# A delta-rule attention with two FFNs on one core: two weights' norms as traces on TensorE, keys and key grams in another form, small products kept together, and a new issue order

## The chip, the cores and the metric

One core of one Trainium2 chip runs the kernel. The metric is device time in microseconds (us), from runs on the chip; the profile is one execution recorded by the hardware profiler. Its engines are called PE (matrix products; PEld is its weight load), DVE (vector operations), ACT (scalar activations), POOL and SP (which issues the DMAs).

## The reference

A delta-rule attention with B = 4, H = 8, S = 768, D = 48 gives x; two FFN layers with 384 → 2048 → 384 follow. Cut to what is computed:

```python
k_n = k / (np.linalg.norm(k, axis=-1, keepdims=True) + 1e-06)
state = np.zeros((B, H, D, D))
for t in range(S):
    y[:, :, t] = einsum('bhd,bhde->bhe', q[:, :, t], state)
    v_old = einsum('bhde,bhd->bhe', state, k_n[:, :, t])
    state += beta[:, :, t, None, None] * einsum('bhd,bhe->bhde', k_n[:, :, t], v[:, :, t] - v_old)
x = y.transpose(0, 2, 1, 3).reshape(B * S, H * D)      # 3072 x 384
h = x @ w_in;  x = np.maximum(0.01 * h, h) @ w_out     # first FFN
h = x @ w2_in; x = (h - np.tanh(h)) @ w2_out           # second FFN
```

## The kernel before

**Work and tiles.** The sequence is cut into 12 chunks `n` of 64 steps; two chunks make a pair `u`. A chunk's attention works on 32 (batch, head) matrices at once: the keys are normalized and transposed (`keys`, `t_batch`: `kf`, `kt`), their gram gives `gd` and `AT` (`g_batch`), 32x32 triangular blocks are inverted on DVE (`inverses`: one stream transpose, then 30 steps of two operations on `xi` and `gd`, then two transposes into `XW`), two rounds of 32x32 products put the corners in (`merges`: products `gd,AT`, `XW,AT`, then `XW,PM`, `PM,gd`), and `queries`, `products`, `states` and `outputs` make the chunk's x. These products are small: 48 or 64 rows by 48 or 64 columns, several of them beside each other in the array, 32 products to a batch. An f32 product goes to PE as two pieces.

**The FFNs.** Each chunk gives 256 tokens. `to_xa` scales them by a power of two from their sum of squares (a norm product `ab,ones` on PE adds over the partitions), splits them into f16 hi and lo, and transposes both. `h_part` makes `ps_h` with three f16 products (hi·hi, hi·lo, lo·hi) per block, ACT and DVE make the activation's halves `g`, `o_part` adds into `ps_o`. `to_xb` does for the second layer what `to_xa` does for the first. The order of layers is 0 and 0 of a pair of chunks, then 1 and 1.

**The weights.** Four weights (0 to 3) are loaded as 64-bit words, unpacked on DVE (`w_f32`, tiles `wi` and `wo`: a shift and two operations of 128x768 for two column blocks), squared with a running sum on ACT (`square_sum` into `wacc`), and, once all 16 blocks are there, scaled by a power of two, `sw` (`pow2_scale`), and split into hi (ACT, then a DMA) and lo (DVE, `wo<-wo,sw,sx`). For weight 0, PE makes the lo half from a scaled unit matrix (`unit_s`) and ACT copies it back. `weight` already has a branch for weights in `TRACE`, which is empty here: it takes the upper 16 bits of the f32 words as bf16,

```python
top = o.bitcast(BF16).rearrange("p (b n w) -> p b n w", n=128, w=2)[:, :, :, 1]
for b in range(w * KT):
    mm(ps, top[:, b], top[:, b], traced == 0, traced == NF * KT - 1)
...
tt(diag, ps, ident, ALU.mult)
dve("tensor_reduce", out=acc[:, 0:1], in_=diag, axis=AX.X, op=ALU.add)
```

so that the diagonal of 48 accumulated 128x128 products holds the sums of squares.

**What sets the order.** All operations are first put into a graph (`put`, `matmul`). `schedule` is a list scheduler: it goes through a model of the engines with costs per instruction, and gives each engine its whole order. Priorities come from the longest tail of work behind an operation plus an offset per stage, the table `BIAS` (some 270 numbers, `("weight", 0, 3)` for a quarter of weight 0's split, and so on). Tiles come from rings of buffers (`sx`, six rooms; `ps_a`, four small PSUM banks; `ps_h` and `ps_o`, two each), and the scheduler lets a tile in when a room is free. On the chip each engine works through its list in order and waits on semaphores. The constants `K_DMA` (chunks whose keys are transposed by DMA), `M8` (pairs whose merges use eight instead of four tiles of the array) and others switch parts on for some chunks.

Of the kernel before, what the change touches and what calls it, by code (L numbers as in the profile page):

```python
# [30 lines left out]
def layers(n):  # L31
# [12 lines left out]
TRACE = ()  # L44
K_SUM = ()
GQ = range(12)
FLIP = range(2, 12)
K_DMA = range(2, 12)
# [19 lines left out]
    ('dma', 'o_part1', 8): -53.43, ('dma', 'o_part1', 9): -2.8, ('dma', 'products', 1): -76.55,  # L68
    ('dma', 'products', 10): -3.83, ('dma', 'products', 2): 25.34, ('dma', 'products', 3): -131.98,
    ('dma', 'products', 4): -6.69, ('dma', 'products', 5): -26.09, ('dma', 'products', 6): 19.17,  # L70
    ('dma', 'products', 7): 77.49, ('dma', 'products', 8): 212.34, ('dma', 'products', 9): 68.97,
    ('dma', 'queries', 0): -146.73, ('dma', 'queries', 1): 17.69, ('dma', 'queries', 10): -116.19,
    ('dma', 'queries', 11): 10.95, ('dma', 'queries', 2): -28.97, ('dma', 'queries', 3): -147.71,
    ('dma', 'queries', 4): -53.56, ('dma', 'queries', 5): 11.09, ('dma', 'queries', 6): -62.06,
    ('dma', 'queries', 7): 5.92, ('dma', 'queries', 8): -44.59, ('dma', 'queries', 9): 63.43,
    ('dma', 'to_xa', 1, 1): -72.81, ('dma', 'to_xa', 10, 1): -8.26, ('dma', 'to_xa', 11, 1): 154.84,
    ('dma', 'to_xa', 2, 1): 2.93, ('dma', 'to_xa', 3, 1): 5.4, ('dma', 'to_xa', 4, 1): 32.04,
    ('dma', 'to_xa', 5, 1): 3.58, ('dma', 'to_xa', 6, 1): 16.44, ('dma', 'to_xa', 7, 1): -144.99,
    ('dma', 'to_xa', 8, 1): -22.03, ('dma', 'to_xa', 9, 1): 22.28, ('dma', 'to_xb', 0, 1): -131.12,
    ('dma', 'to_xb', 1, 1): -169.83, ('dma', 'to_xb', 10, 1): -107.58, ('dma', 'to_xb', 11, 1): 50.71,  # L80
    ('dma', 'to_xb', 2, 1): -7.15, ('dma', 'to_xb', 3, 1): -6.01, ('dma', 'to_xb', 4, 1): -20.2,
    ('dma', 'to_xb', 5, 1): 65.65, ('dma', 'to_xb', 6, 1): -16.83, ('dma', 'to_xb', 7, 1): -97.29,
    ('dma', 'to_xb', 8, 1): 34.46, ('dma', 'to_xb', 9, 1): -4.63, ('dma', 'v', 0): -65.53,
    ('dma', 'weight', 0, 0): -46.39, ('dma', 'weight', 0, 1): -40.51, ('dma', 'weight', 0, 2): -23.2,
    ('dma', 'weight', 0, 3): 21.56, ('dma', 'weight', 0, 4): 56.7, ('dma', 'weight', 0, 5): -5.62,
    ('dma', 'weight', 1, 0): -159.92, ('dma', 'weight', 1, 1): -183.08, ('dma', 'weight', 1, 2): -28.75,
    ('dma', 'weight', 1, 3): -35.61, ('dma', 'weight', 1, 4): -172.45, ('dma', 'weight', 1, 5): -164.56,
    ('dma', 'weight', 2, 0): -32.76, ('dma', 'weight', 2, 1): -6.37, ('dma', 'weight', 2, 2): 4.29,
    ('dma', 'weight', 2, 3): -15.49, ('dma', 'weight', 2, 4): -23.36, ('dma', 'weight', 2, 5): -0.69,
    ('dma', 'weight', 3, 0): 5.74, ('dma', 'weight', 3, 1): -258.17, ('dma', 'weight', 3, 2): -95.47,  # L90
    ('dma', 'weight', 3, 3): -26.22, ('dma', 'weight', 3, 4): 24.43, ('dma', 'weight', 3, 5): -55.49,
# [524 lines left out]
def kernel(  # L616
# [473 lines left out]
    def inv_eng(u):  # L1090
        return INV
# [420 lines left out]
```

## Time and profile before

| | |
|---|---|
| device time, median of 3 runs | 966.23 us (964.88 to 966.59) |
| profiled execution, its own time | 965.78 us |
| its span in the profile | 963.6 us |
| PE busy, products | 896.5 us (93%), 12756 |
| DVE busy, instructions | 608.6 us (63%), 1332 |
| ACT busy, instructions | 499.5 us (52%), 1187 |
| DMA | 71.30 MB, mean 74 GB/s |

The profiled execution's time is 2.2 us above its span, which begins with the first and ends with the last recorded instruction. Busy time is a sum over the span; products of PE overlap, and their ends are modelled.

### The profile page before, as it was taken

The page shows a single profiled execution, that of the slowest core. Times are in us where ns is not written, and L with a number is a line of the kernel's source. Part 1 is how long each engine was busy: PE and PEld are TensorE (multiplying, and loading weights), DVE is VectorE, ACT ScalarE, POOL GpSimd, SP SyncE. Part 2 cuts the span into 40 slices and gives each one's busy share as a digit, 9 for nine tenths or more (in the row PEclk, how much of TensorE's full clock was granted, in tenths as well). Part 3 has the DMA queues.
Part 4 walks back from the last instruction along what each step waited for, and adds up shares of the span by engine and source line. Part 5 has one row for each costly group of instructions (what it writes and reads, how often), then busy time and mean ns, then how long its engine had stood idle before and what let it go on. Part 6 is the DMA issues. An engine that isn't in the chain of part 4 may idle for free.

```text
span 963.6 us, 29002 instructions
## 1 busy us (share of the span) xinstructions
PE 896.5 (93%) x12756; PEld 677.5 (70%) x12756; DVE 608.6 (63%) x1332; ACT 499.5 (52%) x1187; POOL 4.9 (1%) x22
## 2 busy tenths in 40 slices
PE   2346899999999999999999999999999999999997
PEld 2215777778777777777777777777777768777675
DVE  7999999987984458953253598499322344512342
ACT  7657767666357566346362427544334434524342
POOL 1000000000000000000000000000000000000000
PEclk9586799999999999999999999999999999999999
DMA  9983673325022432121012111212021000300000
GB/s 349 402 235 104 193 181 116 108 67 95 23 74 59 71 90 64 21 56 36 18 41 33 55 41 36 50 31 56 17 56 18 3 19 17 52 1 18 17 18 16
DMA packets 86718, 71.30 MB, mean 74 GB/s; under 512 B 61760, under 2 KB 73024, under 8 KB 86592
## 3 DMA queue, kind: packets, MB, share of 16 engines
q1 hardware_dynamic: 86592, 69.46, 27.1%
q8 instruction: 99, 1.62, 0.7%
q14 instruction: 27, 0.22, 0.1%
HBM read 44.14 MB, written 4.72 MB: 51 GB/s over the span
## 4 chain that ended last, share of the span: by engine, by line
PE 79%; DVE 13%; ACT 4%; issue 2%; DMA 1%; SPq 1%; ACTq 0%; DVEq 0%
PE ps_h L609 36%; PE ps_o L609 35%; PE ps_a L609 8%; DVE xi L612 3%; DVE wo L612 3%; DVE wi L612 3%; DVE gd L612 2%; ACT gd L612 1%; DVE g L612 1%; DMA wo<-in_w_in_dram 1%; ACT sx L612 1%; DVE sx L612 1%; ACT XW L612 1%; ACT jk L612 1%; ACT wo L612 1%
## 5 line engine op out<-in xcount | busy, mean ns | idle before, releaser
L609 PE MATMUL ps_h<-x,wi 128*128 128x256 f16 x3456 | 403.6, 273 | 3.1 <-ACT sx L612 2.6
L609 PE MATMUL ps_o<-wo,g 128*128 128x384 f16 x2304 | 400.9, 326 | 0.2 <-issue 0.2
L609 PEld LDWEIGHTS <-wi 128*128 128x128 f16 x3456 | 334.9, 98 | 57.3 <-issue 4.5
L609 PEld LDWEIGHTS <-g 128*128 128x128 f16 x2304 | 221.9, 98 | 132.9 <-issue 0.5
L612 ACT ACTIVATE g<-sx 128x512 f16<-128x512 f32 x192 | 120.3, 628 | 113.0 <-PE ps_o L609 57.6
L612 DVE TENSOR_TENSOR g<-sx,g 128x512 f16<-128x512 f32 x96 | 66.0, 688 | 112.6 <-ACT g L612 112.0
L612 DVE SCALAR_TENSOR_TENSOR sx<-sx,kap,ps_h 128x512 f32<-128x512 f32 x96 | 71.2, 744 | 66.8 <-ACT sx L612 66.3
L612 ACT ACTIVATE sx<-ps_h 128x512 f32<-128x512 f32 x96 | 56.7, 592 | 91.8 <-PE ps_h L609 63.2
L612 ACT ACTIVATE sx<-ps_h,kap 128x512 f32<-128x512 f32 x96 | 65.1, 681 | 73.7 <-PE ps_h L609 63.4
L612 DVE SCALAR_TENSOR_TENSOR g<-sx,g 128x512 f16<-128x512 f32 x96 | 66.0, 688 | 36.4 <-ACT g L612 36.0
L612 DVE TENSOR_TENSOR gd<-xi 128x30 f32<-128x30 f32 (+9 forms) x180 | 59.2, 329 | 3.5
L612 DVE TENSOR_TENSOR xi<-xi,gd 128x30 f32<-128x30 f32 (+9 forms) x180 | 59.1, 329 | 3.5
L612 ACT ACTIVATE jk<-kf 128x48 bf16<-128x48 f32 x160 | 38.4, 240 | 14.3 <-DMA kf<-in_k_dram 10.7
L612 ACT ACTIVATE sx<-x,sxs 128x768 f16<-128x768 f32 (+1 forms) x26 | 22.7, 881 | 22.1 <-DVE sxs L612 22.1
L612 ACT ACTIVATION_READ_ACCUMULATOR jk<-kf 128x1 f32 x160 | 30.0, 187 | 0.0
L612 DVE SCALAR_TENSOR_TENSOR wi<-wo,wi 128x768 int32<-128x768 int32 x32 | 29.8, 950 | 0.0
L609 PE MATMUL ps_a<-q,kt 48*64 48x64 f32 x768 | 15.1, 229 | 13.8 <-DMA q<-in_q_dram 11.4
L612 DVE SCALAR_TENSOR_TENSOR sx<-x,sxs,sx 128x768 f16<-128x768 f32 (+1 forms) x26 | 24.6, 951 | 4.6 <-ACT sx L612 4.4
L612 ACT ACTIVATE sx<-x 128x768 bf16<-128x768 f32 x24 | 20.2, 840 | 13.7 <-DVE x L612 13.4
L612 ACT ACTIVATE gd<-ps_a 32x256 f32<-32x256 f32 (+1 forms) x72 | 23.9, 373 | 5.2 <-PE ps_a L609 4.6
L609 PEld LDWEIGHTS ps_a<-q,kt 48*64 48x64 f32 x768 | 13.3, 142 | 16.6 <-ACT wo L612 11.5
L612 DVE TENSOR_SCALAR sx<-ps_o,kap 128x384 f32<-128x384 f32 x12 | 7.4, 618 | 27.5 <-PE ps_o L609 25.5
(124 smaller groups left out, 730.2 us busy)
## 6 DMA issues: line engine op xcount, KB each, us to landing
wo<-in_w_in_dram SPq DMA_DIRECT2D x32, 384.0 KB, 7.8
q<-in_q_dram SPq DMA_DIRECT2D x12, 512.0 KB, 4.5
wi<-in_w_out_dram SPq DMA_DIRECT2D x14, 384.0 KB, 7.8
kf<-in_k_dram SPq DMA_DIRECT2D x12, 384.0 KB, 3.4
vf<-in_v_dram SPq DMA_DIRECT2D x12, 384.0 KB, 3.4
out_dram<-sx SPq DMA_DIRECT2D x48, 96.0 KB, 2.2
x<-in_w_out_dram SPq DMA_DIRECT2D x10, 384.0 KB, 4.0
b<-in_beta_dram SPq DMA_DIRECT2D x6, 512.0 KB, 4.7
```

The source lines that it names most:

```text
L609: self.eng["pe"].matmul(out=o.real(), lhsT=lhsT.real(), rhs=rhs.real(), start=start, stop=stop)
L612: getattr(self.eng[n.on], op)(**{k: v.real() if isinstance(v, View) else v for k, v in kw.items()})
```

## The change

Two sets and two ranges are changed, and with them the costs and all offsets; some stages are written anew:

- `TRACE = (0, 1)`: the sums of squares of weights 0 and 1 come from 48 products each on PE, in banks of `ps_h` and `ps_o`, a masked multiplication and a sum on DVE; 16 squares each leave ACT, and one instead of 16 small `wacc,ones` products adds over the partitions.
- `K_DMA` begins at 4: chunks 2 and 3 have their keys transposed by PE products with the unit matrix and PSUM copies, as chunks 0 and 1 did, instead of an f16 split, DMA transposes and an addition.
- `PAIRS`: in chunks 4 to 11 the gram of the keys is three f16 products per tile, of the two halves as the DMA left them, instead of one f32 product. The two f16 tiles live until then.
- `to_xa` takes one scale per half of the tokens, from the partition's own sum, so its norm product over the partitions falls away; `to_xb` multiplies it out, `kappa` has one factor less.
- `schedule`: from some point of the model's time on (`t > 250`), where PE is in the small tiles already and FFN products would come next, a small group that is ready and whose instructions are fetched in time goes first.
- `merges` for pairs 0 and 1 goes half by half.
- Costs `SMALL` get two entries, and every number of `BIAS` is new.

`SPLIT`, `BY_PE` and `K_POOL` are empty, so their branches add nothing; they are left out below.

```diff
-TRACE = ()
+PAIRS = range(4, 12)
+TRACE = (0, 1)
-K_DMA = range(2, 12)
+K_DMA = range(4, 12)
...
-    ('weight', 0, 0): -1.81, ('weight', 0, 1): 28.14, ('weight', 0, 2): 11.71, ('weight', 0, 3): -89.58,
...
-        node.cols += o.free * lhsT.shape[0] / 128
+        node.cols += o.free * lhsT.shape[0] / 128 * (4 if lhsT.ap.dtype == F32 and lhsT.shape[0] > 64 else 1)
...
-                kind = 3 if kind else 5
+                kind = 5 if not kind else 6 if lhsT.free > 48 else 7
...
-            if e == "pe" and n.mode:
+            if e == "pe" and n.ffn and mode and t > 250:
+                f = None
+                for x in a:
+                    m = nodes[x[1]]
+                    if not m.mode or gone[x[1]] or f is not None and f < x or not fits(m, t):
+                        continue
+                    c = m.cnt
+                    at = t + (m.warm * left_on / c if c >= left_on else m.warm + (left_on - c) * 0.109)
+                    if page + self.PAGE - at <= self.TURN:
+                        f = x
+                if f is not None:
+                    heappush(a, (p, i, alt))
+                    a.remove(f)
+                    heapify(a)
+                    p, i, alt = f
+                    n = nodes[i]
+            elif e == "pe" and n.mode:
...
-            g_.stage = "weight", i, c // 8
+            g_.stage = "weight", i, c // 8 if c or i else 9
...
             tt(kt.rearrange("p m h i -> p (m h i)"), land[0], land[1], ALU.add)
+            land_t[n] = [t.rearrange("p (m h i) -> p m h i", m=GM, h=2) for t in land]
...
         for m in range(GM):
+            if n in PAIRS:
+                for a, b in ((0, 0), (0, 1), (1, 0)):
+                    for g, h in TILES:
+                        node = mm(ps2[g][HS[h], m], land[a][HD[g], m, h], land[b][HD[g], m, h], a + b == 0, a == 1)
+                continue
...
+            for f in range(2):
+                g_.stage = "merges", u, f
+                for jobs, out in ((first, middle), (second, corner)):
+                    ps = bank(HB)
+                    g_.cut()
+                    for m in range(GM):
+                        for h in range(2):
+                            jobs(ps, m, m + f * GM, HQ[2 * h], HQ[2 * h + 1], *spots(f, h))
+                    out(f, ps)
...
-        if n in BOTH or i:
+        if i:
             copy(w[0], x, scale)
             lo_of(w[1], x, scale, w[0])
         else:
-            for k in range(2):
-                ks = slice(k * KT * 128, (k + 1) * KT * 128)
-                copy(w[0][:, ks], x[:, ks], scale)
-                lo_of(w[1][:, ks], x[:, ks], scale, w[0][:, ks])
+            for k in range(HB2):
+                hi, lo, xk = (rows_of(t)[:, k] for t in (*w, x))
+                copy(hi, xk, scale[:, k:k + 1])
+                lo_of(lo, xk, scale[:, k:k + 1], hi)
...
-        pow2_scale(sx[:, 0:1], squares(x), XT)
-        xa_t[n] = x_turn(n, 0, x, sx[:, 0:1]), sx
+        for k in range(HB2):
+            square_sum(acc[:, k:k + 1], rows_of(x)[:, k], rows_of(junk)[:, k])
+        pow2_scale(sx[:, 0:2], acc, XT, sx[:, 2:4])
+        xa_t[n] = x_turn(n, 0, x, sx[:, 0:2]), sx
...
-            cp(rows_of(x)[:, k], po[k][:, 0:DM].rearrange("p (t f) -> p t f", t=KT))
+            cp(rows_of(x)[:, k], po[k][:, 0:DM].rearrange("p (t f) -> p t f", t=KT), sx[:, 2 + k:3 + k])
```

Three places show how the order moves. Numbers behind names tell tiles of a kind apart; `x2` at the end of a row stands for a product's two pieces or for like instructions in a row. The line of the helper that issues is L612 or L609 before, L634 or L631 after.

On DVE, at the first pair's inverse (`xi_90`, `gd_88`), before: unpacking of weight 0 (`wi_128<-wo_131`) stands between its steps.

```order
L612 TENSOR_TENSOR gd_88<-gd_88,b_110 128x256 x2
L612 SCALAR_TENSOR_TENSOR wi_128<-wo_131,wi_128 128x768
L612 STREAM_TRANSPOSE xi_90<-gd_88 128x32x32
L612 SCALAR_TENSOR_TENSOR wi_128<-wo_131,wi_128 128x768
L612 TENSOR_TENSOR gd_88<-xi_90 128x30
L612 SCALAR_TENSOR_TENSOR wi_128<-wo_131,wi_128 128x768
L612 TENSOR_TENSOR xi_90<-xi_90,gd_88 128x30
L612 SCALAR_TENSOR_TENSOR wi_128<-wo_130,wi_128 128x768
```

After, the first masked products `p_86` come ahead and the inverse's steps follow one another:

```order
L634 SCALAR_TENSOR_TENSOR p_86<-ps_a_97,maskp 128x512
L634 TENSOR_TENSOR gd_88<-gd_88,b_110 128x256
L634 STREAM_TRANSPOSE xi_90<-gd_88 128x32x32
L634 TENSOR_TENSOR gd_88<-xi_90 128x30
L634 TENSOR_TENSOR xi_90<-xi_90,gd_88 128x30
L634 TENSOR_TENSOR gd_88<-xi_90 128x29x2
L634 TENSOR_TENSOR xi_90<-xi_90,gd_88 128x29x2
```

The rest of weight 0's unpacking, and so its scale, moved behind these steps.

On DVE, ahead of the first lo half `g_71` of the FFN, before: blocks of weight 1's lo half (`wo_130<-wo_130,sw`) between the masked products `p_86` and copies of `x_62`.

```order
L612 SCALAR_TENSOR_TENSOR p_86<-ps_a_99,maskp 128x512
L612 SCALAR_TENSOR_TENSOR wo_130<-wo_130,sw,sx_65 128x2x384
L612 SCALAR_TENSOR_TENSOR p_86<-ps_a_98,maskp 128x512
L612 SCALAR_TENSOR_TENSOR wo_130<-wo_130,sw,sx_70 128x2x384
L612 TENSOR_TENSOR x_62<-ps_a_97,x_62 128x2x64
L612 SCALAR_TENSOR_TENSOR wo_130<-wo_130,sw,sx_67 128x2x384
L612 TENSOR_TENSOR x_62<-ps_a_97,x_62 128x256
L612 TENSOR_SCALAR wi_129<-wo_131 128x768
L612 SCALAR_TENSOR_TENSOR wo_130<-wo_130,sw,sx_66 128x2x384
L612 TENSOR_TENSOR g_71<-sx_68,g_71 128x512
```

After, steps of the second inverse (`xi_90`, `gd_89`) stand there, and the masked products come behind the `g`:

```order
L634 SCALAR_TENSOR_TENSOR wo_131<-wo_131,sw,sx_65 128x2x384
L634 TENSOR_TENSOR x_62<-ps_a_97,x_62 128x2x64
L634 TENSOR_TENSOR xi_90<-xi_90,gd_89 128x22x9
L634 TENSOR_TENSOR x_62<-ps_a_97,x_62 128x256
L634 TENSOR_TENSOR gd_89<-xi_90 128x21x10
L634 SCALAR_TENSOR_TENSOR wo_131<-wo_131,sw,sx_70 128x2x384
L634 TENSOR_TENSOR xi_90<-xi_90,gd_89 128x21x10
L634 TENSOR_TENSOR g_71<-sx_67,g_71 128x512
L634 SCALAR_TENSOR_TENSOR p_86<-ps_a_97,maskp 128x512
L634 SCALAR_TENSOR_TENSOR p_86<-ps_a_98,maskp 128x512
```

Four blocks of weight 1's lo half fewer are ahead of the `g`, and 20 steps of the second inverse more.

On PE, late, before: two batches of small products (`u_87,p_86` and `u_87,kf_77`) with nine FFN products between them.

```order
L609 MATMUL ps_a_98<-u_87,p_86 64x48 x2
L609 MATMUL ps_a_99<-u_87,p_86 64x48 x2
L609 LDWEIGHTS wi_128
L609 MATMUL ps_h_92<-x_63,wi_128 128x256
...
L609 MATMUL ps_h_92<-x_63,wi_128 128x256
L609 MATMUL ps_a_98<-u_87,kf_77 48x48
L609 MATMUL ps_a_96<-u_87,kf_77 48x48
```

After, a batch with `u_87,kf_76` follows directly on another, `S_138,q_84`:

```order
L631 MATMUL ps_o_95<-wo_132,g_74 128x384
L631 MATMUL ps_a_99<-S_138,q_84 64x48 x2
...
L631 MATMUL ps_a_96<-S_138,q_84 64x48 x2
L631 MATMUL ps_a_97<-u_87,kf_76 48x48
L631 MATMUL ps_a_98<-u_87,kf_76 48x48
```

A pass from wide products into small ones and back falls away there. In all, PE's list has 64 stretches of small batches from the saturated FFN on before, and 53 after.

## Rows read from the trace of the kernel before

**Rows 1.** The page, its first part: busy time, share of the span, instructions.

```profile
PE 896.5 (93%) x12756; PEld 677.5 (70%) x12756; DVE 608.6 (63%) x1332; ACT 499.5 (52%) x1187; POOL 4.9 (1%) x22
```

**Rows 2.** Windows: length; busy (count) PE, PEld, DVE, ACT, POOL; clock; DMA share; GB/s.

```profile
12.00:111.00 99.00, 53.34 (x1358) 40.01 (x1362) 97.62 (x199) 67.19 (x185) 0.22 (x2) 0.71 0.75 257
111.00:121.00 10.00, 8.61 (x103) 7.39 (x95) 10.00 (x18) 9.66 (x18) 0.00 (x0) 1.00 0.61 198
121.00:958.00 837.00, 834.09 (x11311) 629.96 (x11309) 494.44 (x1092) 415.73 (x963) 0.00 (x0) 1.00 0.21 48
```

**Rows 3.** Waits of PE behind 122 us: total, times, longest.

```profile
PE ps_h L609 <- ACT sx L612: 1.6, 3, 0.9
```

**Rows 4.** The chain that ended last: start us, us, what.

```profile
137.39 5.85 PE ps_o L609 x36
143.24 5.89 PE ps_h L609 x54
```

**Rows 5.** Timeline of PE around the first FFN products.

```profile
111.34 4.10 PE L609 MATMUL ps_h<-x,wi 128*128 128x256 f16 x36
116.50 1.14 PE L609 MATMUL ps_h<-x,wi 128*128 128x256 f16 x9 [1.05 <-ACT sx L612]
...
118.01 3.11 PE L609 MATMUL ps_h<-x,wi 128*128 128x256 f16 x27
120.95 1.14 PE L609 MATMUL ps_o<-wo,g 128*128 128x384 f16 x6
```

**Rows 6.** Timeline of DVE: first inverse, then around the first `g`.

```profile
26.04 2.03 DVE L612 STREAM_TRANSPOSE xi<-gd 128x1024 f32<-128x1024 f32 x1
...
117.17 1.03 DVE L612 SCALAR_TENSOR_TENSOR wo<-wo,sw,sx 128x768 f16<-128x768 f32 x1
118.10 0.70 DVE L612 TENSOR_TENSOR g<-sx,g 128x512 f16<-128x512 f32 x1
118.70 0.97 DVE L612 SCALAR_TENSOR_TENSOR wi<-wo,wi 128x768 int32<-128x768 int32 x1
```

**Rows 7.** Groups by form (last row: the page's own): busy, mean ns, idle before.

```profile
L612 DVE SCALAR_TENSOR_TENSOR wi<-wo,wi 128x768 int32<-128x768 int32 x32 | 29.8, 950 | 0.0
...
L612 DVE TENSOR_TENSOR kt<-sx,sx 128x1024 f32<-128x1024 f16 x10 | 12.2, 1221 | 8.0 <-PE ps_a L609 7.2 <-DMA sx<-KH 0.8
...
L612 DVE TENSOR_TENSOR KH<-kf,KH 128x384 f16<-128x384 f32 x20 | 10.9, 551 | 4.7 <-DMA sx<-KH 3.2 <-ACT KH L612 1.4
...
L612 DVE TENSOR_TENSOR xi<-xi,gd 128x30 f32<-128x30 f32 (+9 forms) x180 | 59.1, 329 | 3.5
```

**Rows 8.** Timeline of PE, late: batches of small products between FFN products.

```profile
229.92 1.16 PE L609 MATMUL ps_a<-q,kt 48*64 48x64 f32 x64
230.90 1.11 PE L609 MATMUL ps_a<-kt 48*64 48x64 f32 x64
...
232.93 0.17 PE L609 MATMUL ps_a<-ab,ones 128*128 128x1 bf16 x1
232.96 1.14 PE L609 MATMUL ps_o<-wo,g 128*128 128x384 f16 x6
234.02 1.16 PE L609 MATMUL ps_a<-kt 48*64 48x64 f32 x64
235.12 1.15 PE L609 MATMUL ps_o<-wo,g 128*128 128x384 f16 x6
```

**Rows 9.** Timeline of PE: the FFN products on either side of 128 corner pieces.

```profile
205.40 1.15 PE L609 MATMUL ps_h<-x,wi 128*128 128x256 f16 x9
...
207.69 0.50 PE L609 MATMUL ps_h<-x,wi 128*128 128x256 f16 x3
```

**Rows 10.** Timeline of PE: pass of weight 0's lo half, first corner product.

```profile
41.14 1.65 PE L609 MATMUL ps_a<-wi,unit_s 128*128 128x384 f32 x2 [2.12 <-ACT unit_s L612]
...
64.47 0.91 PE L609 MATMUL ps_a<-wi,unit_s 128*128 128x384 f32 x2 [1.46 <-ACT wi L612]
...
74.84 0.28 PE L609 MATMUL ps_a<-gd,AT 32*32 32x32 f32 x2 [9.29 <-DVE gd L612]
```

More of the change, by code (lines that the diff above doesn't have):

```diff
@@ new lines @@
+    ('dma', 'grams', 9): -16.61, ('dma', 'k', 0): -51.25, ('dma', 'k', 1): 138.27, ('dma', 'keys', 10): -11.07,
+    ('dma', 'keys', 11): -64.1, ('dma', 'keys', 2): 265.99, ('dma', 'keys', 3): -44.03,
+    ('dma', 'keys', 4): 252.92, ('dma', 'keys', 5): 166.71, ('dma', 'keys', 6): 7.72,
+    ('dma', 'keys', 7): -71.9, ('dma', 'keys', 8): 105.57, ('dma', 'keys', 9): -21.93,
[3 rows of a table added]
+    ('dma', 'o_part1', 8): 10.66, ('dma', 'o_part1', 9): -113.3, ('dma', 'products', 1): -282.81,
+    ('dma', 'products', 10): 20.6, ('dma', 'products', 11): -164.11, ('dma', 'products', 2): 62.48,
@@ L682 @@
     wa_r = ring("wacc", 2, NF)
-    sx_r = ring("sxs", 6, 4)
+    sx_r = ring("sxs", 6, 6)
     kap_r = ring("kap", 2, 4)
@@ L766 @@
     maskb = fixed("maskb", [128, 2], F32)
+    half = fixed("half", [128, 4], F32)
     ones = fixed("ones", [128, 2], BF16)
@@ L1068, in inverses @@
         bs = b_t.pop((u, 0))
[L1069 to L1079 removed]
+        Xf = g_.tile(xi_r, [128, HB * HB + (HB if SPLIT else 0)], F32)
@@ new lines, in inverses, with turned @@
+        X = Xf[:, 0:HB * HB].rearrange("p (i j) -> p i j", i=HB)
+        def turned(o, src):
+            g_.quad = 3
+            n = HB // 2
+            for c in range(2):
+                ps = g_.tile(ps_a, [128, 512], F32).rearrange("p (j i) -> p j i", j=n)
+                g_.cut()
+                for j in range(n):
+                    for q_ in range(4):
+                        mm(ps[HQ[q_], j], src(c * n + j)[HQ[q_]], ident2[HQ[q_], HB * (q_ % 2):HB * (q_ % 2) + HB])
+                cp(o[:, :, c * n:(c + 1) * n], ps.rearrange("p j i -> p i j"))
+            g_.quad = True
@@ new lines, in inverses, with solve @@
+        eng = inv_eng(u)
+        if u in BY_PE:
+            turned(X, lambda j: Gd[:, :, j])
+        else:
+            transpose(X.rearrange("p i j -> p j i"), Gd.rearrange("p m j -> p j m"))
+        if u in SPLIT:
+            n = HB // 2
+            X4 = Xf.rearrange("p (b w) -> p b w", b=2)[:, :, 0:n * HB].rearrange("p b (i j) -> p b i j", j=HB)[:, :, :, 0:n]
+            G1 = Gd.rearrange("p m j -> p (m j)")
+            for j in range(1, n - 1):
+                w = n - j - 1
+                shape = [128, 2, w, j]
+                t = G1[:, 0:2 * w * j].rearrange("p (b i j) -> p b i j", b=2, i=w)
+                tt(t, X4[:, :, j + 1:, j:j + 1].to_broadcast(shape), X4[:, :, j:j + 1, :j].to_broadcast(shape), ALU.mult)
+                tt(X4[:, :, j + 1:, :j], X4[:, :, j + 1:, :j], t, ALU.add)
+        else:
+            def solve(j, lo, hi):
+                col = X[:, lo:hi, j:j + 1].to_broadcast([128, hi - lo, j])
+                tt(Gd[:, lo:hi, :j], col, X[:, j:j + 1, :j].to_broadcast([128, hi - lo, j]), ALU.mult, (eng,))
+                tt(X[:, lo:hi, :j], X[:, lo:hi, :j], Gd[:, lo:hi, :j], ALU.add, (eng,))
+            for j in range(1, HB - 1):
+                solve(j, j + 1, HB)
@@ L1118, in second, with middle @@
             mm(ps[out_dn, m], nat[up, 2 * i + 1], PM[up, i])
-        ps = rounds(first)
-        for f in range(2):
+        xm = tt_.rearrange("p (m a) i -> p a m i", a=2)
+        def middle(f, ps):
             fm = slice(f * GM, (f + 1) * GM)
@@ L1479, in lay_out @@
     low = (np.arange(128) % 32)[:, None, None] > np.arange(32)
+    near = low & ((np.arange(128) % 32)[:, None, None] // 16 == np.arange(32) // 16)
+    low = np.stack([near if u in SPLIT else low for u in range(U)])
     bt = np.concatenate([
```

258 lines of the change are left out of this document (147 added, 111 removed), and 27 rows, old and new, of the table BIAS.

## The prediction

> **What bounds the kernel now.** I read the page first: PE is busy for 93% of the span [rows 1]. A share of the whole says nothing of where the rest lies, so the next view was the windows. It cuts the run in two [rows 2]. From 12 to 111 us DVE works 97.62 of 99.00 us and PE waits for it; from 121 us to the end PE works 834.09 of 837.00 us and DVE only 494.44. The kernel is therefore a start that DVE bounds, and behind it a long stretch that PE bounds. The list of PE's waits after 122 us confirms the second half: its largest entry is 1.6 us [rows 3]. So after the start only PE's own work counts, and a transfer, a copy or a DVE operation that becomes cheaper there is worth nothing.
>
> Of what PE's work consists is read from the chain: 36 `ps_o` products take 5.85 us and 54 `ps_h` products 5.89 us, 162.5 and 109 ns each [rows 4]. 3456 and 2304 of them make 376.7 + 374.4 = 751.1 us. No edit touches these. The small products of the attention that are put between them make 91.8 us, by my count over the 85 places in the timeline where a run of FFN products is broken: the distance from the FFN product before to the one behind, less one FFN step. 120.95 (the first `ps_o`, from where PE no longer pauses) + 751.1 − 7.85 (72 `ps_h` done before) + 91.8 + about 2.8 of waits gives 958.8; PE's last product ends at 958.5 of the 963.6 us, so the account closes.
>
> There are then two levers: when PE saturates, and what the small products cost.
>
> **The start.** The first FFN products run at 111.34, but 36, 9 and 27 of them come with pauses, and PE saturates only at 120.95 with the first `ps_o` [rows 5]. That `ps_o` needs the first lo half `g`, which DVE starts at 118.10 behind a long in-order queue: the step from one start to the next is 0.93 us for a lo block of weight 1 and 0.60 for that `g` [rows 6], each some 0.08 to 0.1 under the row's duration. As DVE hardly pauses, the moment of the first `g` is the sum of what stands ahead of it in DVE's order, plus an offset. I priced every DVE instruction ahead of it by its row's step: 234 instructions and 108.3 us before, 243 and 101.4 after. The offset of the real time to this sum is 8.8 us at the transpose of the first inverse, 26.04 [rows 6], and 9.8 at the first `g`, so the sum is a usable clock. The differences:
> - keys of chunks 2 and 3 go to PE: four `KH` subtractions (0.551, step 0.47) and two `kt` additions (1.221, step 1.14) leave [rows 7]: −4.16.
> - three lo blocks of weight 1 stand ahead instead of seven: −3.74 at 0.93 each.
> - 17 instead of 22 unpacking steps of weight 2 (0.87 for the kind with 0.95 in [rows 7]; others are shorter): −3.56. Both of these are only moved behind the first `g`. They are hidden there if DVE has room, and it has: 494 of 837 us.
> - two masked products `p` −1.20, others −0.34.
> - 20 operations of the second inverse move ahead (mean 0.329 by the page's row [rows 7], the ones here smaller): +4.33; copies of x +0.83; the diagonal and its sum for two weights +0.85.
>
> Together −6.99, so the first `g` starts at about 118.1 − 6.9 = 111.2. The order on PE has 54 `ps_h` ahead of the first `ps_o` instead of 72, so 18 × 0.109 = 1.96 us of work are owed later. Before, the first `ps_o` came 2.85 us behind the start of the first `g`. After, at best it follows the `g`'s own 0.70 (111.9), and 2 us behind it if the second one is late too (113.2). The gain is 120.95 − 1.96 − (111.9 to 113.2) = 5.8 to 7.1 us. I take **−6.0**, the lower part, as a new order on four engines adds some waits that the sum does not know.
>
> The squares of weights 0 and 1 leave ACT (0.84 us each), which is no gain here: ACT is busy for 67 of 99 us [rows 2]. Their 96 products on PE have room in the same stretch (53 of 99 us busy). The 128 products that now transpose the keys of chunks 2 and 3 lie there too. All this I cost at nothing. Without that cover it would be at most 96 × 0.109 (the wider `ps_h` step) + 256 pieces × 0.015 (below) = 14.3 us, or 20 at the clock of 0.71, of which only what lies between two steps of the chain would show.
>
> **The small products late.** A lone batch of 64 pieces (32 f32 products) costs 235.12 − 232.96 − 6 × 0.1625 = 1.185 us, whereas the second of two adjacent ones starts 0.98 us behind the first [rows 8]. Averaged over all such places, batches inside a run cost 0.94 to 0.96 us, and entering and leaving the small tiles together 0.23 us. By these prices, the order of before has 64 such switches and 73.6 us of batches, 88.3 in all (91.8 measured; I use only the difference). The order after has 53, one of them already ahead of the saturation:
> - 12 switches fewer × 0.23: −2.76. The scheduler's new rule takes a ready small group before FFN products when PE is in small tiles already.
> - grams of chunks 4 to 11 as three f16 products: 96 pieces instead of 64 per chunk. No such piece is in the trace. An f32 piece of 64 columns costs 0.96 / 64 = 15 ns. A corner piece of 32 columns costs 8.4 ns: 128 of them lie between nine `ps_h` and the next [rows 9], 207.69 − 205.40 − 9 × 0.109 = 1.31, less one switch, over 128. So the batch costs 0.81 to 1.44 us. An f16 product goes through once where an f32 one needs two pieces, so I take 9 ns, near the lower row: 0.864 against 0.96, eight times: −0.77 (bounds −1.2 and +3.8).
> - 11 or 12 norm sums (`ab,ones`) leave. The next product starts 0.03 us behind the norm's start [rows 8]: −0.3.
>
> Sum **−3.8 us**. Per-half merges, the new rings and `kappa` add no PE work; they decide only what waits.
>
> The sum is −6.0 − 3.8 = −9.8 on the profiled execution's 965.78, so 956.0. The median of the runs lies 0.45 us above the profiled execution, so the forecast is **956.4 us**.
>
> [...] Between matmul starts of small tiles the trace shows 8.4 and 15 ns [rows 8, 9]. [...]
>
> **The rivals.**
> - *The start gains little* (0.15). The sum over DVE's order counts work, not waits. If the transposed keys from PE, a weight's scale or an ACT copy are late by 3 to 5 us, DVE idles and only the late part and some 1 to 2 us remain: 960 to 962. For it speaks that the changed order has DVE operations that depend on PE where before they depended on a DMA; against it that DVE always finds unpacking to do between.
> - *Weight 0's scale comes too late* (0.08, the slower side). In the new order DVE's sum ahead of that scale is 43.8 us instead of 31.7, so the pass that makes the lo halves of weight 0 on PE begins at about 53 instead of 41.14. Before, it took 24.4 us, to 65.5, and the corners of the first merge followed at 74.84 behind 9.29 us of idle PE [rows 10]. With the same length it ends at about 78, where DVE will have the corners' input at some 72 to 74: the corners then wait 4 us in PE's in-order queue, and the first state, the first x and the first `g` with them, as far as DVE cannot fill it. From an end at 84 on (10 us late) the start loses what it gained and what the small products save: 966 to 970. I think the pass gets shorter: its first two products took 1.65 us and two late ones 0.91 [rows 10], and it waited for ACT, which now has no squares of weights 0 and 1.
> - *f16 pieces as dear as f32 ones* (0.08): +4.6 over my value, 961.
> - *f16 pieces have a floor of their own* (0.02): the smallest step of a single matmul that the rows show is 0.03 us, behind the one-column norm sum [rows 8]. At that, 96 pieces take 2.9 us instead of 0.864, eight times: +16, 972. Against it stand the f32 pieces at 15 and 8.4 ns. [...]
> - *Rooms held longer* (0.07). The two f16 tiles of a chunk's keys lie in the ring `sx` of six until PE has made the gram. FFN activations use the same ring. If each of eight chunks adds a wait as long as the longest now, 0.9 [rows 3]: +7, 963.5.
> - *No gain at all* (0.04): waits as large as both terms, 965 to 967.
>
> **How the numbers follow.** The forecast's case has the rest, 0.56, at 952 to 959.5: the start between −4 and −9 us, the small products between −2.5 and −5. The range takes in the first, third and fifth rival: **949 to 964**. About 0.2% (1.9 us) can be told from no change in this kernel. Faster: 0.56 + 0.15 + 0.08 + 0.07 + 0.01 of the late scale = 0.87. Same: 0.03 of the late scale and half of the last rival, 0.05. Slower: 0.04 of the late scale, the floor, and the other half, 0.08.
>
> **What would show it.** In the changed profile: the first DVE `g` at 110 to 113 us and the first `ps_o` right behind; DVE still over 95% busy ahead of it; PE's waits behind the saturation still under 5 us; a gram batch of 96 pieces lengthening PE by 0.8 to 0.9 us; small runs fewer and longer. Wrong would be: long idle of DVE before 110 us, the corners `gd,AT` later than 78 us, `ps_h` waiting for `sx` in many places, or a half clock at the first FFN products.

## The result and the profile after

The changed kernel runs in 954.38 us (median of 4, 953.02 to 954.99), the kernel before in 966.41: a ratio of 0.9877, 95% interval 0.986 to 0.9894, so 11.9 us less. The profiled execution took 953.02 us with a span of 951.3. The forecast was 956.4 in a range of 949 to 964.

The page of the changed kernel, four of its lines (busy time, the slices of DVE and of PE's clock, the instruction queue `q8` with packets, MB and share):

```profile
PE 898.3 (94%) x13194; PEld 684.2 (72%) x13194; DVE 596.4 (63%) x1334; ACT 492.2 (52%) x1193; POOL 4.9 (1%) x22
...
DVE  7999999996984337983598353266943344312432
...
PEclk9587899999999999999999999999999999999999
...
q8 instruction: 103, 1.69, 0.7%
```

Its windows, cut as [rows 2] but by the new times (length; busy and count of PE, PEld, DVE, ACT, POOL; clock; DMA share; GB/s):

```profile
12.00:100.00 88.00, 54.75 (x1377) 43.83 (x1381) 86.65 (x192) 51.96 (x174) 0.00 (x0) 0.71 0.72 258
100.00:121.00 21.00, 18.89 (x312) 15.80 (x307) 21.00 (x50) 19.37 (x48) 0.11 (x1) 0.91 0.66 204
121.00:946.00 825.00, 824.51 (x11517) 624.59 (x11515) 482.03 (x1070) 417.58 (x971) 0.00 (x0) 1.00 0.21 48
```

DVE still fills the start (86.65 of 88.00 us), and PE still fills the rest (824.51 of 825.00). PE's waits behind the saturation: of before, the four that [rows 3] leaves out; then of the changed kernel, all that the view gives behind 114 us:

```profile
PE ps_h L609 <- DVE sx L612: 0.4, 1, 0.4
PE ps_a L609 <- issue: 0.3, 1, 0.3
PE ps_a L609 <- ACT XW L612: 0.3, 1, 0.3
PE ps_o L609 <- issue: 0.2, 1, 0.2
```

```profile
PE ps_h L631 <- DVE sx L634: 0.3, 1, 0.3
```

They were 2.8 us in all with the 1.6 of [rows 3], and are 0.3. "Issue" is time in which PE waits for nothing that the profile shows.

The timeline of PE around the first FFN products answers to [rows 5], the one of DVE to [rows 6]:

```profile
105.47 3.87 PE L631 MATMUL ps_h<-x,wi 128*128 128x256 f16 x27
109.85 1.16 PE L631 MATMUL ps_a<-q,kt 48*64 48x64 f32 x64 [0.51 <-DVE x L634]
110.94 3.12 PE L631 MATMUL ps_h<-x,wi 128*128 128x256 f16 x27
113.90 1.14 PE L631 MATMUL ps_o<-wo,g 128*128 128x384 f16 x6
```

```profile
111.20 0.70 DVE L634 TENSOR_TENSOR g<-sx,g 128x512 f16<-128x512 f32 x1
```

The first `g` starts at 111.20 instead of 118.10, the first `ps_o` at 113.90 instead of 120.95, with 54 instead of 72 `ps_h` products done. PE's last product ends at 946.19 instead of 958.48. Of these 12.29 us the start gives 7.05 − 18 × 0.109 = 5.1, and the stretch behind it 7.2. I took the second apart in both traces as for the forecast. A stretch is what stands between two FFN products; a batch's own price is what it costs where it stands alone, less 0.21 us for going into the small products and back.

| behind the first `ps_o` | before | after |
|---|---|---|
| stretches of small batches, number × 0.21 us | 64, 13.44 | 52, 10.92 |
| their pieces, by the lone batches of either trace | 73.65 | 72.23 |
| what they took beyond that | 2.23 | 0.65 |
| sums for norms and for weights' scales by themselves | 20, 1.94 | 14, 1.15 |
| sum, as measured | 91.26 | 84.95 |

The other 0.9 us are pauses between FFN products.

### The profile page after: what moved, and what is told of

Read it like the earlier page. It is cut to its first block, busy times and chain, and to the rows that moved or that the text cites. A ratio compares the mean times of both kernels' runs of the same rounds, so it can differ in the third digit from the quotient of the medians.

```text
span 951.3 us, 29839 instructions
## 1 busy us (share of the span) xinstructions
PE 898.3 (94%) x13194; PEld 684.2 (72%) x13194; DVE 596.4 (63%) x1334; ACT 492.2 (52%) x1193; POOL 4.9 (1%) x22
## 4 chain that ended last, share of the span: by engine, by line
PE 84%; DVE 10%; ACT 3%; DMA 1%; issue 1%; SPq 1%; ACTq 0%; DVEq 0%
PE ps_h L631 38%; PE ps_o L631 38%; PE ps_a L631 8%; DVE wo L634 2%; DVE wi L634 2%; DVE xi L634 2%; DVE gd L634 2%; ACT sx L634 1%; DMA kf<-in_k_dram 1%; SPq L634 1%; ACT jk L634 0%; ACT XW L634 0%; DVE sx L634 0%; ACT gd L634 0%; DVE p L634 0%
## 5 line engine op out<-in xcount | busy, mean ns | idle before, releaser
L631 PE MATMUL ps_h<-x,wi 128*128 128x256 f16 x3456 | 403.7, 273 | 0.3 <-DVE sx L634 0.3
L631 PE MATMUL ps_o<-wo,g 128*128 128x384 f16 x2304 | 400.3, 326 | 0.0
L631 PEld LDWEIGHTS <-wi 128*128 128x128 f16 (+1 forms) x3504 | 340.2, 98 | 77.5 <-DVE wi L634 22.9
L631 PEld LDWEIGHTS <-g 128*128 128x128 f16 x2304 | 222.5, 98 | 133.0 <-DVE g L634 0.2
L634 ACT ACTIVATE g<-sx 128x512 f16<-128x512 f32 x192 | 120.4, 628 | 97.3 <-DVE sx L634 50.0
L634 DVE TENSOR_TENSOR g<-sx,g 128x512 f16<-128x512 f32 x96 | 66.2, 690 | 108.7 <-ACT g L634 108.4
L634 ACT ACTIVATE sx<-ps_h 128x512 f32<-128x512 f32 x96 | 56.9, 595 | 136.6 <-PE ps_h L631 112.3
L634 DVE SCALAR_TENSOR_TENSOR g<-sx,g 128x512 f16<-128x512 f32 x96 | 66.2, 690 | 63.3 <-ACT g L634 62.9
L634 DVE SCALAR_TENSOR_TENSOR sx<-sx,kap,ps_h 128x512 f32<-128x512 f32 x96 | 71.4, 744 | 54.0 <-ACT sx L634 53.8
L634 ACT ACTIVATE sx<-ps_h,kap 128x512 f32<-128x512 f32 x96 | 65.3, 680 | 33.5 <-PE ps_h L631 21.0
L634 DVE TENSOR_TENSOR gd<-xi 128x30 f32<-128x30 f32 (+9 forms) x180 | 59.6, 331 | 2.6
L634 DVE TENSOR_TENSOR xi<-xi,gd 128x30 f32<-128x30 f32 (+9 forms) x180 | 59.7, 332 | 2.3
L634 ACT ACTIVATE jk<-kf 128x48 bf16<-128x48 f32 x160 | 38.3, 239 | 20.3 <-DMA kf<-in_k_dram 17.0
L634 ACT ACTIVATE sx<-x,sxs 128x384 f16<-128x384 f32 (+1 forms) x36 | 25.5, 715 | 13.6 <-DVE sxs L634 11.3
L634 ACT ACTIVATE gd<-ps_a 32x256 f32<-32x256 f32 (+1 forms) x72 | 23.6, 372 | 15.5 <-PE ps_a L631 15.0
L634 DVE SCALAR_TENSOR_TENSOR wi<-wo,wi 128x768 int32<-128x768 int32 x32 | 30.3, 956 | 0.0
L634 ACT ACTIVATION_READ_ACCUMULATOR jk<-kf 128x1 f32 x160 | 30.0, 188 | 0.0
L634 DVE SCALAR_TENSOR_TENSOR sx<-x,sxs,sx 128x384 f16<-128x384 f32 (+1 forms) x36 | 26.9, 749 | 4.2 <-ACT sx L634 4.1
L631 PE MATMUL ps_h<-wi 128*128 128x128 bf16 x48 | 4.6, 284 | 22.7 <-DVE wi L634 22.7
L634 DVE TENSOR_SCALAR sx<-ps_o,kap 128x384 f32<-128x384 f32 x12 | 7.4, 616 | 29.7 <-PE ps_o L631 29.7
L634 ACT ACTIVATE sx<-x 128x384 bf16<-128x384 f32 (+1 forms) x36 | 22.3, 621 | 6.2 <-DVE x L634 3.8
L634 ACT ACTIVATE x<-ps_o,sxs 128x384 f32<-128x384 f32 x23 | 12.6, 579 | 21.4 <-PE ps_o L631 21.3
```

Source lines behind the costliest of these rows:

```text
L631: self.eng["pe"].matmul(out=o.real(), lhsT=lhsT.real(), rhs=rhs.real(), start=start, stop=stop)
L634: getattr(self.eng[n.on], op)(**{k: v.real() if isinstance(v, View) else v for k, v in kw.items()})
```

## The experiments

Each run is given with its ratio to the kernel before, run on the same chip beside it; the changed kernel's own is 0.9877. All but one change the changed kernel.

**Key grams in f32 again.** The scheduler runs anew; the order is the same up to the first of these grams.

```diff
-PAIRS = range(4, 12)
+PAIRS = ()
```

> The changed kernel with the key grams of chunks 4 to 11 as f32 products again (PAIRS empty); the order is the same up to the first of these grams. Theory: PE is full there, so a chunk costs the difference of a lone batch, 1.185 us (f32, trace of before) less 1.00 us (96 f16 pieces, trace of after): 8 x 0.185 = +1.5 us, 955.9. Rival 1: the f16 tiles held until the gram cost waits elsewhere, then this kernel is as fast or faster, 954.4 or less. Rival 2: f16 pieces cost as much as f32 pieces, then it is 4 us faster.

Measured: 965.74 us, ratio 0.999 (0.9981 to 0.9999), so 11 us slower than the changed kernel, not 1.5. The gram itself explains little of it: the new order has one stretch of 384 pieces that took 13.9 us where its pieces are worth 5.6. Three rows of PE's timeline there:

```profile
536.90 1.15 PE L631 MATMUL ps_a<-vf,XW 64*64 64x48 f32 x64 [0.80 <-DVE vf L634]
539.65 1.15 PE L631 MATMUL ps_a<-u,p 64*64 64x48 f32 x64 [1.61 <-ACT u L634]
...
543.85 1.44 PE L631 MATMUL ps_a<-S,q 48*64 48x48 f32 x44 [1.41 <-issue]
```

PE waits in it for a `vf`, a `u`, and for "issue", that is for nothing that the profile shows. All three numbers that I had written down were wrong, because the undo is not an undo: the scheduler makes another order. What the grams themselves cost is therefore not read from this run.

**A fourth product in these grams.** Here nothing is scheduled anew; the products are put into the finished order.

```diff
     for a, b in ((0, 0), (0, 1), (1, 0)):
         for g, h in TILES:
-            mm(..., land[a][...], land[b][...], a + b == 0, a == 1)
+            mm(..., land[a][...], land[b][...], a + b == 0, False)
+    # into the finished order:
+    for g, h in TILES:
+        mm(..., land[1][...], land[1][...], False, True)
```

> The changed kernel with a fourth f16 product (lo by lo) in each tile of the key grams of chunks 4 to 11, put in behind the third without changing the order of anything: 32 pieces more per chunk, 256 in all. Theory: PE is full, and a piece costs 0.78/96 = 8.1 ns: +2.1 us, 956.5. Rival: pieces cost what f32 pieces do, 15 ns: +3.8 us. Rival: PE's time there is not on the path: 0.

Measured: 968.0 us, ratio 1.0017 (1.0006 to 1.0027), 13.5 us slower. The price of a piece is as expected: a lone gram takes 1.27 us with 128 pieces and 1.00 with 96, 8.4 ns each and 2.1 us for all. The rest stands in one row of PE's waits:

```profile
PE ps_a L631 <- issue: 7.5, 4, 2.1
```

Four stretches of 192 pieces took 1.8 to 2.7 us longer than their pieces are worth, two of them without any gram. What is added shifts every later instruction in PE's queue; the last two kernels of this section test that.

**Without the late rule.** The scheduler runs anew, with the same start.

```diff
-            if e == "pe" and n.ffn and mode and t > 250:
+            if e == "pe" and n.ffn and mode and t > 2500:
```

> The changed kernel without the scheduler's new rule (take a ready small group before FFN products); costs and offsets as they are, the order is the same up to about a quarter of PE's list. Its list has 57 stretches of small batches behind the first ps_o, the changed kernel 52. Theory: 5 switches x 0.21 us = +1.1 us, 955.5, most of the fewer switches came from the offsets. Rival 1: the rule carries the whole late gain: +2.5 us or more. Rival 2: long stretches of small products let the FFN's activations run dry, then it is not slower at all.

Measured: 996.23 us, ratio 1.0304 (1.029 to 1.0318), 42 us slower. Two rows of PE's waits, and four of its timeline in the longest stretch, 705 pieces that took 23.6 us where they are worth 8.7:

```profile
PE ps_a L631 <- issue: 8.3, 6, 3.1
PE ps_h L631 <- DMA x<-sx: 6.8, 1, 6.8
```

```profile
422.65 1.15 PE L631 MATMUL ps_o<-wo,g 128*128 128x384 f16 x6
...
426.32 0.16 PE L631 MATMUL ps_a<-ab,ones 128*128 128x1 bf16 x1 [1.34 <-ACT sx L634]
...
436.57 0.26 PE L631 MATMUL ps_a<-PM,gd 32*32 32x32 f32 x1 [2.76 <-issue]
...
440.01 1.33 PE L631 MATMUL ps_a<-q,kt 48*64 48x64 f32 x37 [1.54 <-DVE S L634]
```

My count of stretches, 57 against 52, said nothing of their length. With these offsets and without the rule, small products pile up until the FFN's next x is late, and then run one behind the other with a wait between each two. The rule and the offsets were fitted to each other, and either without the other lost. That the rule alone carries so many us in some other order is not shown.

**The kernel before with the rule alone.**

```diff
+            if e == "pe" and n.ffn and mode and t > 250:
+                ... (as in the change)
```

> The kernel before with only the scheduler's new rule. Its list has 55 stretches of small batches where before has 64. Theory: 9 x 0.21 = -1.9 us, 964.5. Rival: the gain needs the new offsets, as without them the regrouped products come too late or too early and new waits take it: 966 or more.

Measured: 970.78 us, ratio 1.0037 (1.0024 to 1.005), 3.6 us slower than the kernel before. The rival held. The stretches became fewer as counted, and waits took the gain, among them:

```profile
PE ps_h L625 <- ACT sx L628: 1.6, 3, 0.7
PE ps_a L625 <- DVE S L628: 1.2, 1, 1.2
```

**Eight DVE multiplications in the start.** They write a tile that nobody reads; nothing is scheduled anew.

```diff
+    # into the finished order, ahead of the first transpose on DVE:
+    [tt(extra, ident2, ident2, ALU.mult)] * 8      # 128x512 f32
```

> The changed kernel with eight more DVE multiplications (128x512 f32 into a tile that nobody reads) just ahead of the first inverse's transpose, all other instructions in the same order: about 8 x 0.55 = 4.4 us of DVE time in the start. Theory: DVE bounds the start, so the first g, the saturation of PE and the end all move by 4 to 4.4 us: 958.6. Rival: the start is bound by waits (DMA, PE, ACT), DVE has room, and the time moves by less than 1.5 us.

Measured: 959.15 us, ratio 0.9928 (0.9908 to 0.9947), 4.9 us slower. They took 5.77 us, not the 4.4 that I had priced, and the first `g` came 6.3 us later:

```profile
25.39 5.77 DVE L634 TENSOR_TENSOR extra<-ident 128x512 f32<-128x512 f32 x8
...
117.52 0.69 DVE L634 TENSOR_TENSOR g<-sx,g 128x512 f16<-128x512 f32 x1
```

That is the theory: what is put on DVE in the start comes out at the end, here nearly one for one.

**The same eight in the middle, in one block, and one by one.** The second form puts each between two steps of an inverse.

```diff
+    # in one block, in the stage that turns chunk 6's x:
+    [tt(extra, ident2, ident2, ALU.mult)] * 8
+    # or, in another kernel, one ahead of every fourth step of that inverse
```

> The changed kernel with the same eight DVE multiplications in the middle of the run, in the stage that turns chunk 6's x. Theory: DVE is busy for 482 of 825 us there and PE does not wait for it, so the time stays: 954.4, +0.3 at most for a late g. Rival: DVE's order is tight there too: +2 us or more.

> The changed kernel with the eight DVE multiplications (0.71 us each by the trace of the kernel that had them in one place) in the same stretch of the run as there, but one by one between steps of an inverse, two to four steps apart. Theory: DVE has room on the average, and only a block of 5.8 us ahead of an activation made PE wait (5.6 us, once); spread out they are hidden: 954 to 955.5. Rival: DVE has no room there in any form: +5 us or more.

Measured: 961.74 us in one block, ratio 0.9954 (0.9936 to 0.9972), and 960.59 one by one, ratio 0.9946 (0.9931 to 0.9961): 7 and 6 us slower. Both theories fell, and both rivals held. The longest wait of PE behind 122 us, first for the block, then for the spread:

```profile
PE ps_h L631 <- DVE sx L634: 5.6, 1, 5.6
```

```profile
PE ps_h L631 <- DVE sx L634: 3.5, 1, 3.5
```

The windows of the changed kernel around this place suggest why:

```profile
460.00:480.00 20.00, 20.00 (x310) 16.10 (x308) 14.55 (x37) 10.93 (x23) 0.00 (x0) 1.00 0.15 48
480.00:500.00 20.00, 20.00 (x380) 15.44 (x378) 19.63 (x51) 14.13 (x53) 0.00 (x0) 1.00 0.34 68
500.00:520.00 20.00, 20.00 (x382) 15.12 (x381) 18.31 (x40) 8.52 (x14) 0.00 (x0) 1.00 0.27 62
```

From 480 to 500 us DVE is busy for 19.63 of 20.00 us. It has room over 825 us, but not here, where an inverse, the masked products and the next activation meet. Spread over 22 us around it, the additions end in the same wait, ahead of the same 18 products. In the first kernel the wait does not stand alone:

```profile
498.92 4.00 PE L631 MATMUL ps_h<-x,wi 128*128 128x256 f16 x18 [5.58 <-DVE sx L634]
```

These 18 took 4.00 us, at a granted clock of 0.50, where 18 like them take 2.13. Wait and clock together are the 7 us.

**The offsets of before.** The scheduler runs anew, with all edits but the table.

```diff
-BIAS = {... the new offsets ...}
+BIAS = {... the offsets of the kernel before ...}
```

> The changed kernel with the offsets of the kernel before (stages that did not exist there have none). Its DVE work ahead of the first lo half g sums to 112.6 us (the changed kernel 102.7, the kernel before 108.3), and its list has 58 stretches of small batches. Theory: the offsets carry the whole gain of the start: PE saturates at 121 to 124 us and the time is 964 to 968. Rival: the edits themselves carry it (four key subtractions, two additions, the traces) and the time stays below 960.

Measured: 981.49 us, ratio 1.0157 (1.014 to 1.0173), 27 us slower. The rival fell: the edits without their offsets lose. The theory was too small by 14 us: the first `ps_o` came at 132.49, not at 121 to 124, and the pauses between FFN products grew from 2.0 to 9.9 us. Windows of its start:

```profile
12.00:100.00 88.00, 51.01 (x1042) 38.75 (x1042) 79.44 (x178) 45.22 (x144) 0.11 (x1) 0.70 0.71 256
100.00:121.00 21.00, 13.62 (x393) 12.86 (x394) 20.72 (x36) 14.55 (x31) 0.00 (x0) 0.50 0.62 185
```

DVE is busy for 79.44 of the first 88.00 us there, where the changed kernel has 86.65. The sum of its work misses these waits.

**A longer pass for weight 0's lo half.** Each of its 16 scaled products is done twice; nothing is scheduled anew. In a second kernel, 96 products of the unit matrix by itself are put ahead of the first trace product, where PE is idle, so that PE has 256 instructions more in all.

```diff
+    # in each product group of the pass:
+    mm(ps, unit_s, f32[:, f + j], True, True)
     mm(ps, unit_s, f32[:, f + j], True, False)
     mm(ps, unit[:, 1], w[:, j], False, True)
+    # second kernel only, ahead of the first trace product, into its bank:
+    [mm(ps, unit, unit, True, True)] * 96
```

> The changed kernel with each of the 16 scaled products of weight 0's pass on PE done twice, all else in the same order: some 10 us more for PE between 54 and 73 us, where the pass ends 0.7 us ahead of the first corner product. Theory: the corners of the first merge wait in PE's queue behind the pass, and DVE has little to do that does not need them, so most of it comes out at the end: +5 to +10 us, 959 to 964. Rival: DVE's other work covers it, and the time moves by less than 2 us.

> The changed kernel with weight 0's scaled products on PE done twice, as before, and 96 products of the unit matrix ahead of the first trace product, so that both together are 256 PE instructions more, a whole packet. Theory: without the shift that kernel lost 26 us, of which some 8 came from the pass itself (first g at 119.3 instead of 111.2) and the rest from stretches of small products that were moved within their packets; with the shift only the 8 remain: 961 to 964. Rival: the pass costs the whole 26 us: 978 or more.

Measured: 980.51 us without the shift, ratio 1.0146 (1.0118 to 1.0174), and 963.49 with it, ratio 0.9974 (0.9965 to 0.9984). The first corner product of either kernel, and PE's largest wait behind 122 us in the first:

```profile
82.80 0.21 PE L631 MATMUL ps_a<-gd,AT 32*32 32x32 f32 x1 [0.41 <-ACT wi L634]
```

```profile
PE ps_a L631 <- issue: 9.7, 6, 1.9
```

```profile
84.18 0.21 PE L631 MATMUL ps_a<-gd,AT 32*32 32x32 f32 x1 [0.41 <-ACT wi L634]
```

The corner stood at 73.89; the pass moves it by 8.9 and 10.3 us. In the first kernel the first `ps_o` comes 8.5 us later, in the second, which has the added products too, 10.6, and the second ends 9.4 us later than the changed kernel. So the pass costs about what it moves the corners by, and the other 17 us of the first kernel are waits on issue (12.5 us in 9 places), and what follows them, which the shift takes away.

**The shift by itself.** 64 or 128 products of the unit matrix in that place, with nothing else changed.

```diff
+    # into the finished order, ahead of the first trace product, into its bank:
+    [mm(ps, unit, unit, True, True)] * 64          # or 128
```

> The changed kernel with 64 products of the unit matrix by itself (128 PE instructions with their weight loads) ahead of the first trace product, into a bank that the trace overwrites; PE is idle there for 22.7 us, and every other instruction keeps its order. PE's instruction queue brings packets of 16.4 KB (1.69 MB in 103), which is some 256 instructions, so the long stretches of small products now begin half a packet away from where they did. Theory: the late gain rests on where such a stretch lies within a packet; PE then waits on issue for 1.7 to 2.7 us in several of its stretches of 160 to 192 pieces, as in the kernel with grams of four, and the time is 962 to 972. Rival: those waits came from something else in the kernels that showed them (more work in the gram, later x), and the time stays within 1 us of 954.4.

> The same with 128 such products (256 PE instructions, a whole packet). Theory: the stretches lie within a packet as they did, so there are no new waits on issue, and the time is 954 to 956, although PE has twice as many products more than with half a packet. Rival: the added products themselves cost (they delay the trace, or change the clock): the time is above that with half a packet.

Measured: 969.42 us with 64, ratio 1.0037 (1.0018 to 1.0057), and 956.19 with 128, ratio 0.9895 (0.9877 to 0.9912). The larger addition is 13 us faster, and within 2 us of the changed kernel (its first `ps_o` comes 2.7 us later, that of the half packet 2.2). PE's waits behind 117 us, of the half packet and then all of the whole one:

```profile
PE ps_a L631 <- issue: 7.5, 5, 2.0
```

```profile
PE ps_o L631 <- DVE g L634: 0.5, 1, 0.5
```

The whole one has one packet more than the changed kernel, 104 instead of 103, and its stretches take 84.9 us in all, as the changed kernel's do, the half packet's 95.1. In the kernel with half a packet, the timeline around one stretch of 192 pieces, and windows through it:

```profile
456.43 2.13 PE L631 MATMUL ps_h<-x,wi 128*128 128x256 f16 x18
...
462.25 1.12 PE L631 MATMUL ps_a<-S,kt 48*64 48x48 f32 x33 [1.88 <-issue]
463.31 2.10 PE L631 MATMUL ps_h<-x,wi 128*128 128x256 f16 x9
```

```profile
458.00:460.00 2.00, 2.00 (x154) 1.73 (x154) 0.12 (x1) 1.38 (x3) 0.00 (x0) 1.00 0.00 0
460.00:462.00 2.00, 0.37 (x27) 0.25 (x19) 0.58 (x1) 1.94 (x6) 0.00 (x0) 1.00 0.03 8
462.00:464.00 2.00, 1.75 (x37) 1.47 (x38) 0.58 (x1) 0.81 (x3) 0.00 (x0) 0.59 0.05 8
464.00:466.00 2.00, 2.00 (x11) 1.26 (x10) 1.57 (x3) 0.00 (x0) 0.00 (x0) 0.56 0.00 0
466.00:468.00 2.00, 2.00 (x16) 1.36 (x15) 0.00 (x0) 0.00 (x0) 0.00 (x0) 1.00 0.00 0
```

The stretch lasts 4.92 us instead of 2.39: PE is busy for 0.37 of the 2.00 us from 460 on. And it costs more than its wait, as the granted clock falls to 0.59 and 0.56 for the 4 us after, where nine `ps_h` take 2.10 us instead of 1.14 [rows 5]. That is not so behind each of the five waits. Behind those of 1.88 and 1.46 us the clock fell (to 0.50 to 0.65); behind those of 1.98, 1.37 and 0.84 it stayed at 1.00, here the first of these:

```profile
290.00:292.00 2.00, 0.94 (x60) 0.76 (x46) 1.02 (x2) 1.67 (x4) 0.00 (x0) 1.00 0.27 51
292.00:294.00 2.00, 1.08 (x33) 0.97 (x34) 0.44 (x1) 0.00 (x0) 0.00 (x0) 1.00 0.03 8
```

The traces also say where PE waits. Count its matmuls and weight loads from the start of the kernel: behind the first `ps_o`, the changed kernel's variants have 27 waits on issue, in six kernels, and each stands 174 to 180 above a multiple of 256. By the counts, 13194 products and as many weight loads in 103 packets, a packet holds 128 products with their loads, so this is one place in the packet, from which I infer that it is a packet that PE waits for. 128 small ones in a row take 1.1 to 1.9 us in the traces of the kernel before and of the changed one, while behind 118 us no two packets of any trace start less than 3.25 us apart. In the half packet's kernel six stretches reach over two such places, and five of them wait at the second; in the changed kernel and with a whole packet none reaches over two.

## Why the prediction was right

The total came within 2 us with some luck, as two misses partly offset each other: the start gained 0.9 us less than forecast, the rest 3.4 us more.

**What bounds.** Right on the average: the start moves with DVE (4.9 us for 5.77 of work), and behind it PE is busy for 824.51 of 825.00 us. One premise was too wide: that DVE has room behind the saturation because it works only 494 of 837 us. Eight more operations around 480 to 500 us cost 6 to 7 us.

**The start, −6.0.** The mechanism was right, the size near: −5.1. The sum over DVE's order gave the first `g` at 111.2, and it came at 111.20. What was off is the step from there to the first `ps_o`: I had 0.7 to 2.0 us, it took 2.70, as 27 `ps_h` still ran when the `g` was ready. So they did before, from 118.01 to 120.95 [rows 5], when the step was 2.85: it hung on PE's order, not on the `g`. The sum is a clock only where the order fits the waits. With the offsets of before the sum put the first `g` at about 121 and it came at 129.57, behind 8.6 us in which DVE idled between 12 and 100 us.

**Weight 0's scale.** The scale came at 53.55, as expected (53), and the pass ran from 54.33 to 73.2, 18.8 us instead of 24.4, so the rival did not come true. The first corner waited for a copy of that pass.

```profile
54.33 1.59 PE L631 MATMUL ps_a<-wi,unit_s 128*128 128x384 f32 x2
...
72.34 0.81 PE L631 MATMUL ps_a<-wi,unit_s 128*128 128x384 f32 x2
...
73.89 0.21 PE L631 MATMUL ps_a<-gd,AT 32*32 32x32 f32 x1 [0.41 <-ACT wi L634]
```

The longer pass shows that there is hardly any cover behind it: +10.3 us at the corner were +9.4 at the end. The rival's price for a pass that ends near 84 us was therefore about right, and "as far as DVE cannot fill it" had next to no effect; the time there was 963.5 instead of 966 to 970, as the small products had gained more than I forecast.

**The small products, −3.8.** The switches were right (−2.5 for 12). One term was mis-sized. A gram of 96 f16 pieces costs 0.79 us, not 0.864, as the FFN products around a lone one show,

```profile
219.83 1.14 PE L631 MATMUL ps_o<-wo,g 128*128 128x384 f16 x6
...
221.81 1.15 PE L631 MATMUL ps_o<-wo,g 128*128 128x384 f16 x6
```

221.81 − 219.83 − 6 × 0.1625 = 1.00 with its switch, where the f32 one took 1.185: −1.5 for eight, not −0.77. The rival of a floor for f16 pieces, 0.03 us each, fell with it: 8.4 ns a piece, by the run with a fourth product in these grams. The lone sums gave −0.8, not −0.3, but that is not the norms: 18 lone `ab,ones` became 12 at 0.03 each, −0.2, and the other 0.6 lie in one group of `wacc,ones` for a weight's scale, at 178.59 before, which cost 1.02 us there, 0.43 of it a wait for DVE, and costs 0.41 now. And "they decide only what waits" stood for nothing in my sum, while what stretches took beyond their pieces went down by 1.6 us and the pauses between FFN products by 0.9, 2.5 in all. That is the step that failed by the most, and on the lucky side: no run shows which edit took these waits away.

**Rooms held, and no gain.** Neither shows: no wait of PE for an activation's room behind 114 us beyond the one row above.

**What I left out.** The forecast has no rival for PE's instruction queue. I had costed keeping small products together as a pure gain of 0.21 to 0.23 us a switch. The runs show that a stretch of 192 pieces, 384 instructions in 2.4 us, runs through or waits up to 2.1 us by its place in the packets, several times per run. At most 0.5 us of the measured gain is of this kind, as the kernel before lost no more to such waits; for the rest it is a loss that the changed order, with more long stretches, avoids. How it does so stands in `schedule` of both kernels: its model counts 128 products to a packet (`left_on`), lets the next one come 3.4 us after the last at the earliest (`PAGE`), and puts FFN products first where a small group would have to wait. It does not always succeed: the changed kernel's variants that were scheduled anew have 1.6 to 8.3 us of such waits. Products that are put into its finished order move all that follows away from the places that it chose, and half a packet of them cost five times what 12 switches save. How much a single one of these edits contributes stays open: every undo that was scheduled anew (the grams, the rule, the offsets) lost more than the whole gain or nearly all of it.

## What to carry to other kernels

In an order that a scheduler has fitted closely, an edit's worth cannot be read by undoing it and scheduling again; put the edit into the finished order instead, and keep the number of instructions ahead of long stretches of short ones the same, modulo a packet of the instruction queue (here 128 products with their weight loads: 64 products more cost 15 us, 128 more 2). A control whose additions make up a whole packet separates the cost of the added work from the cost of moving what follows. Busy time averaged over a long stretch is no cover: look at the 20 us in which the work would lie.

## What the runs showed of the hardware

- The instruction queue `q8` brought 103 packets of 16.4 KB in the changed kernel. That they are PE's is inferred from the counts: 26388 matmuls and weight loads in 103 packets are 256 each, and 256 more made 104 packets. Half a packet of harmless products cost 13 us more than a whole one. The changed kernel has no wait of PE on issue behind 114 us. In its variants, stretches of 160 to 192 small products waited on issue, up to 2.0 us at once with half a packet (five of the six that reach over two of the places above) and up to 2.1 us with a fourth product in the grams.
- No two of these packets started less than 3.25 us apart behind 118 us in any of the traces (3.42 in the changed kernel's, 3.45 in that of before).
- Such a wait can be paid twice: in the half packet's kernel, behind 1.88 us without products, the granted clock was 0.56 to 0.59 for about 4 us. Behind three of the five waits of that kernel, one of them 1.98 us long, it stayed at 1.00.
- An f16 piece of 64 columns in a quarter of the array costs 8.4 ns (32 more of them made a lone gram 0.27 us longer), an f32 piece of as many columns 15 (64 of them took 0.98 us [rows 8]).
